# A second expert tile prepared during attention, and the expert totals moved behind a quarter of a layer

## The chip, the core and the metric

The kernel runs on one core of one Trainium2 chip. The metric is the device time of one execution in microseconds. Its parts are named as in the profile: PE (TensorE's matmuls) and PEld (its weight loads), DVE (VectorE), ACT (ScalarE), POOL (GpSimd) and SP (SyncE), which issues most DMA transfers.

## What is computed

Attention with pooled queries, followed by a mixture of experts of which each token takes one:

```python
B, H, S, D = 8, 8, 1152, 64
q_pool = q.reshape(B, H, S // 2, 2, D).mean(axis=3)
scores = matmul(q_pool, k.T) / sqrt(D)
attn = softmax(scores)                      # max subtracted, exp, sum
x = matmul(attn, v)  ->  4608 tokens x 512
logits = x @ w_gate                         # 8 experts
e = argmax(logits);  gate = softmax(logits)[e]
eom = sigmoid(x @ w_output_gate)[e]
out = gate * eom * (relu(x @ w1[e]) @ w2[e])    # 512 -> 1024 -> 512
```

## The kernel before

**Attention** walks over 32 pairs of heads (8 batches of 4 pairs) in an order written out by hand for PE, DVE, ACT and POOL. When a batch of 576 tokens is complete, its router runs in small steps spread between the matmuls (`router`, L396 to L486): it takes the argmax, works out each token's slot in its expert's list, adds the batch's counts to `cum` (L473), writes the rows of x to the DRAM table `xrows` (L461, L462) and scatters the tokens' ids into the DRAM lists `idscr`, one list for each expert (L477). For the last batch this router is the end of attention: nothing is left to hide it, and its chain of small DVE operations runs from L323 through L377, L389 and L414 to L473.

**One tile ahead.** A tile is up to 256 tokens of one expert. Behind the router of the sixth batch (`b == nb - 3`, L485) `setup` (L628) looks at the counts so far. It picks the fullest expert, which is sure to hold 256 tokens, and gathers the ids (L612) and rows (L623) of a full tile of that expert by indirect DMA on POOL. This is tile -1. `oh1` marks its expert, `es` holds its number for the weight load. The loads of two weight buffers are issued before attention ends: the buffer `raw1a`, `raw2a` takes the weights of that expert, read from a register, and the buffer `raw1b`, `raw2b` takes expert 0's weights, as a guess for tile 0 (L718 to L723). A set of weights is four transfers of 1024 KB.

**The experts** (`run`, L668). 22 tiles are run one after the other: tile -1, then tiles 0 to 20, sorted by expert. With these inputs the experts get 157, 587, 936, 411, 612, 525, 663 and 717 tokens. Three more tiles stand in a conditional tail (L917), which isn't reached. A tile (`tile_`, L870) goes through these steps, and inside the block of L905 PE, DVE and ACT keep the order in which it is written:

- four times: `split2` makes a quarter of the high and low parts of the second layer's weights (L739 on ACT, L740 on DVE); `l1` runs a quarter of the first layer: 24 matmuls (L764), the ReLU on ACT (L767), the remainder on DVE (L768); then one function of the list `todo` is run;
- the weights of tile t + 2 are loaded into the buffer that this tile used (`loads`, L725), on a condition: only where the expert of that buffer changes (`chg`);
- `split1` for the next tile (L733, L734), half of the second layer (`l2`, 24 matmuls, L776 to L778), the next tile's transposes (`xt`: L749 on PE, L751 on ACT, L752 on DVE), the other half of the second layer. Outputs are scaled on DVE (L782) and scattered by POOL (L783).

Outside that block and between it and attention, the framework orders by priority and readiness, so an instruction of the expert block can run between instructions of attention. The first tile's transposes have high priority (L898).

**The totals.** What tiles 0 and up hold depends on the final `cum`. `totals1` (L791) copies `cum` on DVE (L793) and sums it over the partitions by a matmul on PE (L795). `totals2` (L797) turns the counts into tile numbers, less the tile that was taken early. `totals3` (L825) makes each tile's expert (`ei`), the flags `chg` and the positions `ri` in the id lists (L839). `first` (L858) then gathers ids and rows for tiles 0 and 1 and issues the load of tile 0. `totals1` and `totals2` run ahead of tile -1, `totals3` and `first` behind its first two quarters.

Of the kernel before, what the change touches and what calls it, by code (L numbers as in the profile page):

```python
# [8 lines left out]
F32 = mybir.dt.float32  # L9
# [23 lines left out]
TS = 256  # L33
# [13 lines left out]
XW = 513  # L47
# [524 lines left out]
def keep_tiles(tc, kp, NT):  # L572
    nc = tc.nc
    k = {}

    def t(name, shape, dt):
        k[name] = kp.tile(shape, dt, name=name)
        return k[name]
    make_identity(nc, t('ident', [128, 128], F32))
    nc.vector.memset(t('ones', [128, 128], BF16), 1.0)  # L580
    nc.vector.memset(t('onesf', [128, 128], F32), 1.0)
    nc.gpsimd.iota(t('em8', [128, 5, 8], F32), pattern=[[0, 5], [1, 8]], base=-8, channel_multiplier=0, allow_small_or_imprecise_dtypes=True)
    nc.gpsimd.iota(t('Tn', [128, NT, 8], F32), pattern=[[1, NT], [0, 8]], base=0, channel_multiplier=0, allow_small_or_imprecise_dtypes=True)
    nc.gpsimd.iota(t('Tp', [128, NT, 2], F32), pattern=[[TS, NT], [128, 2]], base=0, channel_multiplier=1, allow_small_or_imprecise_dtypes=True)
    nc.gpsimd.iota(t('e46', [128, 8], F32), pattern=[[ESTRIDE, 8]], base=0, channel_multiplier=0, allow_small_or_imprecise_dtypes=True)
    t('oh1', [128, 8], F32)
    t('ef', [128, NT + 2], F32)
    t('es', [128, 1], I32)
    return k


class Moe:
    def __init__(self, tc, kp, keep, xrows, idscr, cum, w1, w2, out, nb):
        self.tc, self.kp, self.keep = tc, kp, keep
        self.xrows, self.idscr, self.cum, self.out = xrows, idscr, cum, out
        self.NTOK = nb * NQ
        self.early = max(nb - 2, 0) * NQ
        self.P1 = -(-self.early // 8) // TS
        self.NT = (self.NTOK - 8) // TS + 8 - self.P1
        assert self.P1 <= 1  # L600
        self.w1v = w1.rearrange("e (c p) f -> e p c f", p=128)
        self.w2v = w2.rearrange("e (c p) f -> e p c f", p=128)
        self.T = {}
        self.scat = []
# [14 lines left out]
    def gather(self, t, pool, bufs, rows):  # L619
        nc = self.tc.nc  # L620
        for j in range(2):
            xg = pool.tile([128, XW], F32, name="xg", bufs=2 * bufs)
            self.lastg = nc.gpsimd.indirect_dma_start(out=xg, out_offset=None, in_=self.xrows[0:rows],  # L623
                                         in_offset=bass.IndirectOffsetOnAxis(ap=self.T[t]['ids'][j][:, 0:1], axis=0),
                                         bounds_check=rows - 1, oob_is_err=False)
            self.T[t]['xg'].append(xg)

    def setup(self, psum):  # L628

        nc, kp, k, P1 = self.tc.nc, self.kp, self.keep, self.P1  # L630
        V = nc.vector
        if not P1:
            V.memset(k['oh1'], 0.0)
            V.memset(k['ef'][:, 0:2], 0.0)
            return
        cb = kp.tile([128, 8], BF16, name="cb1")
        V.tensor_copy(out=cb, in_=self.cum)
        yield
        yield 1
        cp = psum()  # L640
        nc.tensor.matmul(cp[:, 0:8], lhsT=k['ones'], rhs=cb, start=True, stop=True)
        cn = kp.tile([128, 8], F32, name="cn1")
        V.tensor_copy(out=cn, in_=cp[:, 0:8])
        yield
        mx = kp.tile([128, 1], F32, name="mx1")
        em = k['em8'][:, 0]
        V.tensor_reduce(out=mx, in_=cn, axis=AX.X, op=ALU.max)
        V.tensor_tensor(out=cn, in0=cn, in1=mx.broadcast_to([128, 8]), op=ALU.is_equal)
        yield
        V.tensor_tensor(out=cn, in0=cn, in1=em, op=ALU.mult)  # L650
        V.tensor_reduce(out=mx, in_=cn, axis=AX.X, op=ALU.min)
        yield
        V.tensor_scalar(out=k['ef'][:, 1:2], in0=mx, scalar1=8.0, scalar2=None, op0=ALU.add)
        V.tensor_tensor(out=k['oh1'], in0=em, in1=mx.broadcast_to([128, 8]), op=ALU.is_equal)
        V.memset(k['ef'][:, 0:1], 0.0)
        yield
        V.tensor_copy(out=k['es'], in_=k['ef'][:, 1:2])
        ri = kp.tile([128, 2], U32, name="ri1")
        rb = kp.tile([128, 1], F32, name="rb1")
        V.tensor_scalar(out=rb, in0=k['ef'][:, 1:2], scalar1=float(ESTRIDE), scalar2=None, op0=ALU.mult)  # L660
        V.tensor_tensor(out=ri, in0=k['Tp'][:, 0], in1=rb.broadcast_to([128, 2]), op=ALU.add)
        yield
        self.gather_ids(-1, ri, kp, 1)
        for _ in range(8):
            yield
        self.gather(-1, kp, 1, self.early)

    def run(self):  # L668
        tc, k, P1, NT = self.tc, self.keep, self.P1, self.NT
# [2 lines left out]
        with ExitStack() as ctx:  # L672
# [42 lines left out]
                        tc.add_manual_dep(d.ins, behind.ins.name, mybir.DependencyInfo(mybir.DependencyClass.Sync, mybir.DependencyReason.DATA), reason="small transfers first")  # L715
                return r[-1]

            if P1:  # L718
                e = nc.sync.value_load(k['es'][0:1, 0:1], min_val=0, max_val=7)
                wload(0, bass.ds(e, 1))  # L720
            else:
                wload(0, slice(0, 1))
            lastw = [wload(1, slice(0, 1))]  # L723

            def loads(t, **kw):  # L725
                with tc.issue_after(lastw[0].ins):
                    e = nc.sync.value_load(z['ei'][0:1, t:t + 1], min_val=0, max_val=7)
                    c = nc.sync.value_load(z['chg'][0:1, t:t + 1], min_val=0, max_val=1)
                    lastw[0] = wload((t + 1) % 2, bass.ds(e, 1), cond=c, cond_hint=False, **kw)

            def split1(t, c):
                raw = raw1[(t + 1) % 2]
                nc.scalar.copy(out=W1[0][:, c], in_=raw[:, c])  # L733
                V.tensor_tensor(out=W1[1][:, c], in0=raw[:, c], in1=W1[0].bitcast(F32)[:, c], op=ALU.subtract)  # L734

            def split2(t, c):
                z = slice(2 * c, 2 * c + 2)
                raw = raw2[(t + 1) % 2]
                nc.scalar.copy(out=W2[0][:, z], in_=raw[:, z])  # L739
                V.tensor_tensor(out=W2[1][:, z], in0=raw[:, z], in1=W2[0].bitcast(F32)[:, z], op=ALU.subtract)  # L740

# [55 lines left out]
            def totals2():  # L797
                cp = z['cp']
                ni = m1.tile([128, 8], I32, name="ni")
                V.scalar_tensor_tensor(out=ni, in0=k['oh1'], scalar=-float(TS) * P1, in1=cp[:, 0:8], op0=ALU.mult, op1=ALU.add)  # L800
                ns = m1.tile([128, 8], I32, name="ns")
                V.tensor_scalar(out=ni, in0=ni, scalar1=TS - 1, scalar2=None, op0=ALU.add)
                V.tensor_scalar(out=ns, in0=ni, scalar1=8, scalar2=None, op0=ALU.logical_shift_right)
# [11 lines left out]
                ts = z['ts'] = m1.tile([128, 8], F32, name="ts")  # L815
                V.tensor_tensor(out=ts, in0=te, in1=nt, op=ALU.subtract)
                eo = m1.tile([128, 8], F32, name="eo")
                V.scalar_tensor_tensor(out=eo, in0=k['oh1'], scalar=float(TS) * P1, in1=k['e46'], op0=ALU.mult, op1=ALU.add)
                vA = z['vA'] = m1.tile([128, 8], F32, name="vA")
                V.scalar_tensor_tensor(out=vA, in0=ts, scalar=-float(TS), in1=eo, op0=ALU.mult, op1=ALU.add)  # L820

# [34 lines left out]
                    self.gather(t, mg, 3, self.NTOK + 1)  # L856

            def first():  # L858
                for t in range(2):
                    gid(t)  # L860
                loads(0)
                for t in range(2):
                    gat(t)
                z['lg'] = self.lastg
                if not P1:
                    loads(1, behind=z['lg'])

            order = list(range(-P1, NT - SKIP))

# [23 lines left out]
            E = mybir.EngineType  # L893
            for c in range(4):
                split1(order[0], c)
            todo = [totals2, totals3, first]
            if P1:
                with tc.high_priority():  # L898
                    xt(order[0])
            else:  # L900
                totals1()
                while todo:
                    todo.pop(0)()
                xt(order[0])
            with tc.manual_schedule(engines={E.PE, E.DVE, E.Activation}):  # L905
                if P1:
                    totals1()
                    todo.pop(0)()
                for i, t in enumerate(order):
                    tile_(i, t, order[i + 1] if i + 1 < len(order) else None)  # L910
                pend.pop(0)()
# [5 lines left out]
            with tc.If(rv > NT - SKIP):  # L917
                for t in tail:
                    gid(t)
                    gat(t)  # L920
                    e = nc.sync.value_load(z['ei'][0:1, t:t + 1], min_val=0, max_val=7)
                    wload((t + 1) % 2, bass.ds(e, 1))
                    for c in range(4):
                        split1(t, c)
                    xt(t)
                    for c in range(4):
                        split2(t, c)
                    for g in range(4):
                        l1(t, g)
                    for j in range(2):  # L930
                        l2(t, j)()


def body(tc, qT, kT, vL, wg, w1, w2, out, nb=8):
    nc = tc.nc
    NTOK = nb * NQ
    with tc.tile_pool(name="dram", bufs=1, space=bass.MemoryType.DRAM) as dp, tc.tile_pool(name="keep", bufs=1) as kp:
# [6 lines left out]

        def init(i):
            if i == 0:
                dz = kp.tile([1, XW], F32, name="dz")
                nc.gpsimd.memset(dz, 0.0)
                nc.sync.dma_start(out=xrows[NTOK:NTOK + 1], in_=dz)
                nc.gpsimd.memset(di, NTOK)  # L950
# [39 lines left out]
```

## Time and profile before

| | us |
|---|---|
| median of 3 runs (1623.79 to 1625.01) | 1624.14 |
| profiled run | 1624.72 |
| its span, first to last instruction | 1622.7 |
| PE busy | 1533.1 |
| DVE, ACT, POOL busy | 1073.4, 1078.5, 996.3 |
| last matmul of the last router (L444) starts at | 1087.33 |
| first layer of tile -1 starts at | 1091.20 |
| first layer of tile 0 starts at | 1121.65 |

The mean granted TensorE clock was 0.986. In a line of a timeline stand the start in us from the span's start, the length in us (for several in a row, from the first to the end of the last), the engine, the line, the operation, the tile written and those read, the shape, the count, and in brackets how long the engine stood idle before and what ended it. A matmul's length is its passage through the array; how fast they follow one another is read from their starts. A line of waits gives who waited, for whom, the total, the count and the longest.

### The profile page before, as it was taken

The page shows a single profiled execution, that of the slowest core. Times are in us where ns is not written, and L with a number is a line of the kernel's source. Part 1 is how long each engine was busy: PE and PEld are TensorE (multiplying, and loading weights), DVE is VectorE, ACT ScalarE, POOL GpSimd, SP SyncE. Part 2 cuts the span into 40 slices and gives each one's busy share as a digit, 9 for nine tenths or more (in the row PEclk, how much of TensorE's full clock was granted, in tenths as well). Part 3 has the DMA queues.
Part 4 walks back from the last instruction along what each step waited for, and adds up shares of the span by engine and source line. Part 5 has one row for each costly group of instructions (what it writes and reads, how often), then busy time and mean ns, then how long its engine had stood idle before and what let it go on. Part 6 is the DMA issues. An engine that isn't in the chain of part 4 may idle for free. (4 is left out here: it accounts for less than half of the span.)

```text
span 1622.7 us, 42199 instructions
## 1 busy us (share of the span) xinstructions
PE 1533.1 (94%) x16618; PEld 1411.1 (87%) x16618; DVE 1073.4 (66%) x2222; ACT 1078.5 (66%) x1862; POOL 996.3 (61%) x917
## 2 busy tenths in 40 slices
PE   4999999999999999999999999879999999999997
PEld 4898889888988888888888888868999999999996
DVE  4676776776676676676677767656666566656663
ACT  2887778877878787878777877744445444544541
POOL 4887888788879788879788978634222322232300
PEclk9999999999999999999999999979999999999999
DMA  7765455655566457446645664255454655263600
GB/s 207 217 160 143 133 149 149 156 139 141 152 151 158 124 144 189 129 123 175 158 129 153 161 154 127 83 173 196 168 190 156 213 176 194 94 226 107 208 22 25
DMA packets 88754, 245.48 MB, mean 151 GB/s; under 512 B 13082, under 2 KB 17370, under 8 KB 88546
## 3 DMA queue, kind: packets, MB, share of 16 engines
q1 hardware_dynamic: 78826, 221.07, 48.6%
q0 software_dynamic: 9728, 21.67, 4.2%
q8 instruction: 134, 2.20, 0.6%
q14 instruction: 66, 0.54, 0.1%
HBM read 165.04 MB, written 23.81 MB: 116 GB/s over the span
## 5 line engine op out<-in xcount | busy, mean ns | idle before, releaser
L233 DVE TENSOR_REDUCE pm<-mp 128x1 f32<-128x384 f32 x864 | 457.6, 549 | 263.3 <-PE mp L232 257.7
L295 POOL TENSOR_TENSOR pl<-p,ph 128x576 f16<-128x576 f32 x381 | 490.2, 1287 | 187.8 <-ACT ph L294 155.5
L232 PE MATMUL mp<-ka,qa 128*128 128x384 f32 x960 | 317.7, 347 | 20.2 <-DMA qa<-yq 18.5
L293 ACT ACTIVATE p<-sps 128x576 f32<-128x576 f32 x381 | 251.0, 659 | 116.8 <-PE sps L281 108.3
L308 PEld LDWEIGHTS <-ph 128*128 128x128 f16 x2880 | 262.6, 97 | 74.3 <-DVE xb L323 40.8
L308 PE MATMUL av<-vt,ph 128*128 128x65 f16 x2880 | 297.0, 194 | 23.4 <-DVE xb L323 23.4
L279 PE MATMUL sps<-qa,ka 128*128 128x288 f32 x1152 | 281.6, 326 | 16.7 <-ACT ph L294 10.9
L309 PE MATMUL av<-vt,ph 128*128 128x64 f16 x2880 | 294.7, 195 | 0.0
L310 PE MATMUL av<-vt,pl 128*128 128x65 f16 x2880 | 293.8, 193 | 0.0
L309 PEld LDWEIGHTS <-ph 128*128 128x128 f16 x2880 | 266.2, 97 | 0.4
L310 PEld LDWEIGHTS <-pl 128*128 128x128 f16 x2880 | 266.5, 99 | 0.0
L232 PE MATMUL mp<-kb,qb 66*128 66x384 f32 x768 | 262.5, 342 | 0.6 <-DMA kb<-kp 0.6
L281 PE MATMUL sps<-qb,kb 68*128 68x288 f32 x1152 | 248.5, 298 | 2.8 <-DMA qb<-mr 2.8
L294 ACT ACTIVATE ph<-sps 128x576 f16<-128x576 f32 x381 | 249.3, 654 | 0.0
L279 PEld LDWEIGHTS sps<-qa,ka 128*128 128x128 f32 x1152 | 183.5, 191 | 27.9 <-ACT ph L294 19.2
L764 PE MATMUL hps<-xh,w1h 128*128 128x256 f32 x704 | 200.4, 285 | 0.0
L764 PE MATMUL hps<-xl,w1h 128*128 128x256 f32 x704 | 200.3, 284 | 0.0
L232 PEld LDWEIGHTS mp<-ka,qa 128*128 128x128 f32 x960 | 180.4, 192 | 22.8 <-issue 18.5
L764 PE MATMUL hps<-xh,w1l 128*128 128x256 f32 x704 | 199.6, 284 | 0.0
L767 ACT ACTIVATE hh<-hps 128x512 fp32r<-128x512 f32 x88 | 52.7, 598 | 221.1 <-PE hps L764 221.1
L285 ACT ACTIVATE ph<-sps 128x576 f16<-128x576 f32 x195 | 128.9, 661 | 92.0 <-PE sps L281 89.7
L281 PEld LDWEIGHTS sps<-qb,kb 68*128 68x128 f32 x1152 | 186.7, 191 | 3.2 <-DMA qb<-mr 3.2
(170 smaller groups left out, 3184.6 us busy)
## 6 DMA issues: line engine op xcount, KB each, us to landing
ka<-xk SPq DMA_DIRECT2D x128, 288.0 KB
raw1b<-in_w_dram SPq DMA_DIRECT2D x24, 1024.0 KB
raw2b<-in_w_dram SPq DMA_DIRECT2D x24, 1024.0 KB
raw1a<-in_w_dram SPq DMA_DIRECT2D x22, 1024.0 KB
raw2a<-in_w_dram SPq DMA_DIRECT2D x22, 1024.0 KB
qp<-in_qT_dram SPq DMA_DIRECT2D x32, 576.0 KB
kpf<-in_kT_dram SPq DMA_DIRECT2D x32, 576.0 KB
vp<-in_vL_dram SPq DMA_DIRECT2D x32, 576.0 KB
```

Source lines behind the costliest of these rows:

```text
L232: nc.tensor.matmul(mp, lhsT=l, rhs=r, start=j == 0, stop=j == len(ops) - 1)
L233: nc.vector.tensor_reduce(out=pm[:, i:i + 1], in_=mp, axis=AX.X, op=ALU.max)
L279: nc.tensor.matmul(sps[:, j, 0:288], lhsT=ka[:, h, ks], rhs=qa[:, o + 288 * j:o + 288 * j + 288], start=True, stop=False)
L281: nc.tensor.matmul(sps[:, j, 0:288], lhsT=kb[:, h, ks], rhs=qb[:, h, 288 * j:288 * j + 288], start=False, stop=True)
L285: nc.scalar.activation(out=ph2, in_=x, func=AF.Exp, scale=1.0 / 16)
L293: nc.scalar.activation(out=p32.rearrange("p (j n) -> p j n", j=2), in_=x, func=AF.Exp, scale=1.0 / 16)
L294: nc.scalar.activation(out=ph2, in_=x, func=AF.Exp, scale=1.0 / 16)
L295: nc.gpsimd.tensor_tensor(out=pl, in0=p32, in1=ph, op=ALU.subtract)
L308: nc.tensor.matmul(av_[:, qb, 0:65], lhsT=hi, rhs=vt[:, h, c, 0:65], start=c == 0 and qb == 0, stop=False)
L309: nc.tensor.matmul(av_[:, qb, 0:64], lhsT=hi, rhs=vt[:, h, c, 66:130], start=False, stop=False)
L310: nc.tensor.matmul(av_[:, qb, 0:65], lhsT=lo, rhs=vt[:, h, c, 0:65], start=False, stop=c == NC - 1 and qb == 4)
L764: nc.tensor.matmul(hp[:, f], lhsT=W1[w][:, c, fs], rhs=d[x][:, c], start=i == 0, stop=i == 11)
```

## The change

Two tiles, numbered -2 and -1, are prepared in attention. `setup` picks the fullest expert, takes 256 from its count, picks the fullest of what is left, and gathers ids and rows of both, each with eight steps between ids and rows. With these inputs they are experts 2 and 7. Both weight buffers are loaded by register, so the guess of expert 0 is gone, and tile 0's weights come by a conditional load like all others. That load, `loads(0)`, now stands at the end of tile -2's first layer and waits for the last gather that `first` issued. `first` gathers tile 0 alone. The numbers of tiles go from 24 to 23 in the tables, and the tiles run are -2 to 19, again 22, with the same contents in sum. `totals1` becomes the first entry of `todo`, so `totals1`, `totals2`, `totals3` and `first` stand behind the first, second, third and fourth quarter of tile -2's first layer. A row of zeros (`dz`) shares the buffers of the early rows.

```diff
-        self.P1 = -(-self.early // 8) // TS
+        self.P1 = sum(self.early - TS * i >= 8 * TS for i in range(2))
...
         cp = psum()
         nc.tensor.matmul(cp[:, 0:8], lhsT=k['ones'], rhs=cb, start=True, stop=True)
...
+        for i in range(2):
+            V.tensor_reduce(out=mx, in_=cn[i], axis=AX.X, op=ALU.max)
+            V.tensor_tensor(out=w, in0=cn[i], in1=mx.broadcast_to([128, 8]), op=ALU.is_equal)
+            yield
+            V.tensor_tensor(out=w, in0=w, in1=em, op=ALU.mult)
+            V.tensor_reduce(out=mx, in_=w, axis=AX.X, op=ALU.min)
+            yield
+            V.tensor_scalar(out=k['ef'][:, i:i + 1], in0=mx, scalar1=8.0, scalar2=None, op0=ALU.add)
+            V.tensor_tensor(out=oh[i], in0=em, in1=mx.broadcast_to([128, 8]), op=ALU.is_equal)
+            yield
+            if i == 0:
+                V.scalar_tensor_tensor(out=cn[1], in0=oh[0], scalar=-float(TS), in1=cn[0], op0=ALU.mult, op1=ALU.add)
...
-        self.gather_ids(-1, ri, kp, 1)
-        for _ in range(8):
-            yield
-        self.gather(-1, kp, 1, self.early)
+        for i in range(2):
+            self.gather_ids(i - 2, ri[i], kp, 2)
+            for _ in range(8):
+                yield
+            self.gather(i - 2, kp, 2, self.early)
+            yield
...
-            if P1:
-                e = nc.sync.value_load(k['es'][0:1, 0:1], min_val=0, max_val=7)
-                wload(0, bass.ds(e, 1))
-            else:
-                wload(0, slice(0, 1))
-            lastw = [wload(1, slice(0, 1))]
+            lastw = [None]
+            for i in range(2):
+                e = slice(0, 1)
+                if P1:
+                    e = bass.ds(nc.sync.value_load(k['es'][0:1, i:i + 1], min_val=0, max_val=7), 1)
+                lastw[0] = wload(i, e)
...
             def first():
-                for t in range(2):
+                for t in range(1 if P1 else 3):
                     gid(t)
-                loads(0)
-                for t in range(2):
+                for t in range(1 if P1 else 3):
                     gat(t)
                 z['lg'] = self.lastg
                 if not P1:
-                    loads(1, behind=z['lg'])
+                    loads(0)
+                    loads(1)
...
-            todo = [totals2, totals3, first]
+            todo = [totals1, totals2, totals3, first]
...
             with tc.manual_schedule(engines={E.PE, E.DVE, E.Activation}):
-                if P1:
-                    totals1()
-                    todo.pop(0)()
                 for i, t in enumerate(order):
                     tile_(i, t, order[i + 1] if i + 1 < len(order) else None)
```

More of the change, by code (lines that the diff above doesn't have):

```diff
@@ L587, in keep_tiles @@
     t('ef', [128, NT + 2], F32)
-    t('es', [128, 1], I32)
+    t('es', [128, 2], I32)
     return k
@@ L597, in __init__ @@
         self.early = max(nb - 2, 0) * NQ
-        self.P1 = -(-self.early // 8) // TS
+        self.P1 = sum(self.early - TS * i >= 8 * TS for i in range(2))
         self.NT = (self.NTOK - 8) // TS + 8 - self.P1
-        assert self.P1 <= 1
+        assert self.P1 in (0, 2)
         self.w1v = w1.rearrange("e (c p) f -> e p c f", p=128)
@@ L621, in gather @@
         for j in range(2):
-            xg = pool.tile([128, XW], F32, name="xg", bufs=2 * bufs)
+            xg = pool.tile([128, XW], F32, name="xg", tag="xg", bufs=2 * bufs)
             self.lastg = nc.gpsimd.indirect_dma_start(out=xg, out_offset=None, in_=self.xrows[0:rows],
@@ L641, in setup @@
         nc.tensor.matmul(cp[:, 0:8], lhsT=k['ones'], rhs=cb, start=True, stop=True)
-        cn = kp.tile([128, 8], F32, name="cn1")
-        V.tensor_copy(out=cn, in_=cp[:, 0:8])
+        cn = [kp.tile([128, 8], F32, name=f"cn{i}") for i in range(2)]
+        V.tensor_copy(out=cn[0], in_=cp[:, 0:8])
         yield
+        em = k['em8'][:, 0]
+        es8 = k['e46']
+        oh = [kp.tile([128, 8], F32, name=f"ob{i}") for i in range(2)]
+        w = kp.tile([128, 8], F32, name="cw")
         mx = kp.tile([128, 1], F32, name="mx1")
-        em = k['em8'][:, 0]
@@ L647, in setup @@
-        V.tensor_reduce(out=mx, in_=cn, axis=AX.X, op=ALU.max)
-        V.tensor_tensor(out=cn, in0=cn, in1=mx.broadcast_to([128, 8]), op=ALU.is_equal)
-        yield
-        V.tensor_tensor(out=cn, in0=cn, in1=em, op=ALU.mult)
-        V.tensor_reduce(out=mx, in_=cn, axis=AX.X, op=ALU.min)
-        yield
-        V.tensor_scalar(out=k['ef'][:, 1:2], in0=mx, scalar1=8.0, scalar2=None, op0=ALU.add)
-        V.tensor_tensor(out=k['oh1'], in0=em, in1=mx.broadcast_to([128, 8]), op=ALU.is_equal)
-        V.memset(k['ef'][:, 0:1], 0.0)
@@ L656, in setup @@
[L656 to L662, printed above, removed]
-        self.gather_ids(-1, ri, kp, 1)
-        for _ in range(8):
+        rb = kp.tile([128, 1], F32, name="rb1")
@@ new lines, in setup @@
+        ri = [kp.tile([128, 2], U32, name=f"ri{i}") for i in range(2)]
+        for i in range(2):
[10 more added lines that the diff above has]
+                V.scalar_tensor_tensor(out=cn[1], in0=oh[0], scalar=-float(TS), in1=cn[0], op0=ALU.mult, op1=ALU.add)
+                V.tensor_tensor(out=w, in0=oh[0], in1=es8, op=ALU.mult)
+            else:
+                V.scalar_tensor_tensor(out=w, in0=oh[0], scalar=float(TS), in1=es8, op0=ALU.mult, op1=ALU.add)
+                V.tensor_tensor(out=w, in0=oh[1], in1=w, op=ALU.mult)
+            yield
+            V.tensor_reduce(out=rb, in_=w, axis=AX.X, op=ALU.add)
+            V.tensor_tensor(out=ri[i], in0=k['Tp'][:, 0], in1=rb.broadcast_to([128, 2]), op=ALU.add)
+            yield
@@ L665, in setup @@
+        V.tensor_tensor(out=k['oh1'], in0=oh[0], in1=oh[1], op=ALU.add)
+        V.tensor_copy(out=k['es'], in_=k['ef'][:, 0:2])
+        yield
+        for i in range(2):
+            self.gather_ids(i - 2, ri[i], kp, 2)
+            for _ in range(8):
+                yield
+            self.gather(i - 2, kp, 2, self.early)
             yield
-        self.gather(-1, kp, 1, self.early)
     def run(self):
@@ L728, in loads @@
                     c = nc.sync.value_load(z['chg'][0:1, t:t + 1], min_val=0, max_val=1)
-                    lastw[0] = wload((t + 1) % 2, bass.ds(e, 1), cond=c, cond_hint=False, **kw)
+                    lastw[0] = wload(t % 2, bass.ds(e, 1), cond=c, cond_hint=False, **kw)
             def split1(t, c):
-                raw = raw1[(t + 1) % 2]
+                raw = raw1[t % 2]
                 nc.scalar.copy(out=W1[0][:, c], in_=raw[:, c])
@@ L737, in split2 @@
                 z = slice(2 * c, 2 * c + 2)
-                raw = raw2[(t + 1) % 2]
+                raw = raw2[t % 2]
                 nc.scalar.copy(out=W2[0][:, z], in_=raw[:, z])
@@ L799, in totals2 @@
                 ni = m1.tile([128, 8], I32, name="ni")
-                V.scalar_tensor_tensor(out=ni, in0=k['oh1'], scalar=-float(TS) * P1, in1=cp[:, 0:8], op0=ALU.mult, op1=ALU.add)
+                V.scalar_tensor_tensor(out=ni, in0=k['oh1'], scalar=-float(TS), in1=cp[:, 0:8], op0=ALU.mult, op1=ALU.add)
                 ns = m1.tile([128, 8], I32, name="ns")
@@ L817, in totals2 @@
                 eo = m1.tile([128, 8], F32, name="eo")
-                V.scalar_tensor_tensor(out=eo, in0=k['oh1'], scalar=float(TS) * P1, in1=k['e46'], op0=ALU.mult, op1=ALU.add)
+                V.scalar_tensor_tensor(out=eo, in0=k['oh1'], scalar=float(TS), in1=k['e46'], op0=ALU.mult, op1=ALU.add)
                 vA = z['vA'] = m1.tile([128, 8], F32, name="vA")
@@ L905, in run @@
             with tc.manual_schedule(engines={E.PE, E.DVE, E.Activation}):
-                if P1:
-                    totals1()
-                    todo.pop(0)()
                 for i, t in enumerate(order):
@@ L921, in run @@
                     e = nc.sync.value_load(z['ei'][0:1, t:t + 1], min_val=0, max_val=7)
-                    wload((t + 1) % 2, bass.ds(e, 1))
+                    wload(t % 2, bass.ds(e, 1))
                     for c in range(4):
@@ L946, in init @@
             if i == 0:
-                dz = kp.tile([1, XW], F32, name="dz")
+                dz = kp.tile([128, XW], F32, name="dz", tag="xg", bufs=4)[0:1]
                 nc.gpsimd.memset(dz, 0.0)
```

## The prediction

> **What bounds the kernel now.** I read the page first, for the span, then PE's waits in the expert part alone, then PE's, DVE's and ACT's timelines across the change-over from attention to experts.
>
> ```profile
> span 1622.7 us, 42199 instructions
> ```
>
> The profiled run took 1624.72 us, of which 1622.7 is the span, so 2.0 lie around it. It is 0.58 above the median of the runs, 1624.14.
>
> ```profile
> engine line waited for: us in total, times, longest us
> PE cp L795 <- DVE cb L793: 3.6, 1, 3.6
> PE xps L749 <- DMA xg<-xrows,ids: 2.4, 2, 1.6
> ```
>
> These are all the waits of PE from 1088 us to the end. The 22 tiles are bound by PE, and weights and splits cost nothing there. So what the change can win after attention lies in these two places, with the clock that drops around them. Both kernels run 22 tiles: by the counts of the inputs the eight experts fill 22 tiles however many full ones are taken early, and the conditional tail isn't reached. I take all later tiles as unchanged.
>
> ```profile
> 1091.15 0.19 PE L795 MATMUL cp<-cb,ones 128*128 128x8 bf16 x1 [3.63 <-DVE cb L793]
> 1091.20 0.56 PE L764 MATMUL hps<-xh,w1h 128*128 128x256 f32 x1
> 1091.56 0.41 PE L764 MATMUL hps<-xl,w1h 128*128 128x256 f32 x1
> ...
> 1096.25 0.41 PE L764 MATMUL hps<-xh,w1l 128*128 128x256 f32 x1
> 1096.46 0.41 PE L764 MATMUL hps<-xh,w1h 128*128 128x256 f32 x1
> ...
> 1105.42 0.40 PE L776 MATMUL yp<-w2h,hh 128*128 128x512 f32 x1
> ...
> 1111.81 0.66 PE L749 MATMUL xps<-ident,xg 128*128 128x128 f32 x4 [0.77 <-DMA xg<-xrows,ids]
> 1114.09 0.98 PE L749 MATMUL xps<-ident,xg 128*128 128x128 f32 x4 [1.62 <-DMA xg<-xrows,ids]
> ...
> 1121.65 0.28 PE L764 MATMUL hps<-xh,w1h 128*128 128x256 f32 x1
> ```
>
> The first tile: the totals' matmul, the first layer from 1091.20 (its second quarter begins at 1096.46), the second layer from 1105.42, the next tile's transposes with their two waits, the next tile from 1121.65.
>
> **Part 1: the totals move behind the first quarter.** The 3.63 us look like the prize. But what else held the first layer?
>
> ```profile
> 1089.68 1.28 DVE L752 TENSOR_TENSOR xl<-xps,xh 128x512 fp32r<-128x512 f32 x2
> 1090.87 0.22 DVE L793 COPY cb<-cum 128x8 bf16<-128x8 bf16 x1
> ```
> ```profile
> 1087.72 1.05 ACT L751 CAST xh<-xps 128x512 fp32r<-128x512 f32 x2
> ```
>
> The first tile's own `xl` is finished by DVE at 1089.68 + 1.28 = 1090.96, and every second matmul of the layer needs it or comes behind one that does. L793 ends at 1091.09 and L795 starts 0.06 later; with the same 0.06 behind `xl`, the layer's second matmul could start at 1091.02 in place of 1091.56. The first one needs only `xh`, ready at 1088.77, and goes ahead. Gain 0.54; if the first doesn't go ahead, 0.36 later, 0.18. I take 0.54.
>
> Now the price of the new place. In the written order of DVE the copy L793 stands behind L768 of the first quarter, which waits for ACT's L767, which waits for that quarter's 24 matmuls; and PE, in order, holds the second quarter behind L795.
>
> ```profile
> 1096.84 0.60 ACT L767 ACTIVATE hh<-hps 128x512 fp32r<-128x512 f32 x1 [8.06 <-PE hps L764]
> ```
> ```profile
> 1097.47 0.69 DVE L768 SCALAR_TENSOR_TENSOR hl<-hps,hh 128x512 fp32r<-128x512 f32 x1 [2.82 <-ACT hh L767]
> 1098.07 0.35 DVE L829 TENSOR_TENSOR ge<-Tn,tb 128x192 f32<-128x192 f32 x1
> ```
>
> The 24th matmul starts at 1096.25, L767 at 1096.84, L768 at 1097.47, the next DVE operation at 1098.07. With the copy there (0.22), the 0.06, and the 0.05 from L795 to the next matmul, the second quarter starts at 1098.40 instead of 1096.46: a new wait of 1.94 us. It depends on no cover that I could lose; all three links are in this trace. Behind PE's wait stands all of PE's queue; behind the copy on DVE stand only the totals and L740 of the next quarters, which l2 needs some 10 us later.
>
> DVE's first instruction of the expert block is now L740 of the first quarter, 1.23 us long, no longer held behind the totals. It may run before the router's end:
>
> ```profile
> 1077.09 1.03 ACT L739 CAST w2h<-raw2a 128x1024 fp32r<-128x1024 f32 x1
> 1082.02 0.76 ACT L374 CAST xh<-tp 128x256 fp32r<-128x256 f32 x3 [3.90 <-PE tp L370]
> ```
> ```profile
> 1080.94 0.49 DVE L323 TENSOR_TENSOR xb<-av,r 128x320 f32<-128x320 f32 x1
> 1082.43 0.95 DVE L377 TENSOR_TENSOR xl<-tp,xh 128x256 fp32r<-128x256 f32 x3 [0.99 <-ACT xh L374]
> 1093.42 1.23 DVE L740 TENSOR_TENSOR w2l<-raw2a,w2h 128x1024 fp32r<-128x1024 f32 x1
> ```
>
> ACT already does so: L739 of the tile runs ahead of the router's L374, in a stretch that was idle. In DVE's idle 0.99 before L377, L740 would delay the router's chain by 1.23 - 0.99 = 0.24; between two links of the chain by 1.23; behind L752 by nothing. I take 0.24, by ACT's example.
>
> **Part 2: the clock behind the new wait.** The stretches below give, behind their length, the busy time of PE, PEld, DVE, ACT and POOL, the granted clock, the DMA share and GB/s.
>
> ```profile
> 1090.27:1093.68 3.41, 2.53 (x12) 2.54 (x13) 2.88 (x17) 0.00 (x0) 2.78 (x3) 0.50 1.03 250
> 1093.68:1097.10 3.42, 3.42 (x17) 3.42 (x17) 0.97 (x1) 0.26 (x1) 2.50 (x2) 0.50 0.22 55
> 1097.10:1100.51 3.41, 3.41 (x30) 3.41 (x30) 2.81 (x10) 1.93 (x4) 0.00 (x0) 0.98 0.01 1
> ```
>
> The clock changes here on a grid of 3.41 us. The stretch with PE busy for 2.53 did not bring full clock, the one with 3.42 did. Matmuls go at 0.213 us at half clock (1091.56 to 1096.46 holds 23).
>
> ```profile
> 1565.01 0.28 PE L764 MATMUL hps<-xh,w1h 128*128 128x256 f32 x1
> 1576.52 0.40 PE L776 MATMUL yp<-w2h,hh 128*128 128x512 f32 x1
> 1588.32 0.28 PE L764 MATMUL hps<-xh,w1h 128*128 128x256 f32 x1
> ```
>
> At full clock the layer's 96 take 11.51, 0.120 each. So each us at half clock costs 1 - 0.120 / 0.213 = 0.44. The changed kernel resumes at about 1096.46 - 0.54 + 0.24 + 1.94 = 1098.1; before, only the 0.64 from 1096.46 to 1097.10 were slow (0.28 lost). On this grid full clock comes at 1100.51 or 1103.92, after 2.4 or 5.8 us: 0.77 or 2.27 more lost than before. If instead the first quarter already brings full clock, about nothing is lost. Where the grid falls differs from run to run, so I take 1.2 between 0 and 2.3. [...]
>
> **Part 3: two tiles in attention.** The second prepared tile needs no gather at the change-over. From the second layer's start to the next tile the profile has 1121.65 - 1105.42 = 16.23, against 1588.32 - 1576.52 = 11.80 late in the run: 4.43 go, the two waits and the half clock they brought. What is late next? The gather for tile 0, now needed one tile later, at about 1137 us:
>
> ```profile
> 1100.34 0.21 DVE L839 TENSOR_TENSOR ri<-A,Tp 128x48 uint32<-128x48 f32 x1
> ```
> ```profile
> ids<-idscr,ri POOLq DMA_INDIRECT x44, 2.4
> xg<-xrows,ids POOLq DMA_INDIRECT x44, 3.7
> ```
>
> The positions were ready at 1100.34; with the totals one piece and one wait later, I put them at about 1111; two id gathers, two row gathers and a landing (some 8 us) make it 1119. Expert 0's weights, loaded statically before and now read behind that gather, start then:
>
> ```profile
> 1117.58:1120.99 3.41, 3.41 (x17) 2.81 (x16) 1.23 (x1) 1.05 (x1) 2.66 (x3) 0.98 0.98 336
> ```
>
> At 336 GB/s their 4.2 MB (four transfers of 1024 KB) need 12.5 us, so 1131.5, when the splits of that tile begin at about 1132 and its first layer at 1143. The load is hidden, and slack is left if it takes half as long again.
>
> In attention the change adds four indirect transfers on POOL and some 13 small DVE operations.
>
> ```profile
> 765.16:800.16 35.00, 33.80 (x457) 31.52 (x456) 24.27 (x56) 28.84 (x56) 28.20 (x25) 1.00 0.60 151
> 895.00:930.00 35.00, 33.80 (x455) 31.28 (x455) 26.00 (x65) 28.77 (x56) 31.92 (x28) 1.00 0.64 163
> ```
>
> The second stretch holds today's preparation, the first is the same place one batch earlier: PE's 33.80 is equal. Cost 0, covered by POOL's and DVE's slack.
>
> **Sum:** -0.54 + 0.24 + 1.94 + 1.2 - 4.43 = -1.6. Ends: -0.54 + 0 + 1.94 + 0 - 4.43 = -3.0, and -0.18 + 1.23 + 1.94 + 2.3 - 4.43 = +0.9. Against the profiled run 1623.1; its 0.58 above the median taken off, **1622.5** (1621.1 to 1625.0).
>
> **Rivals.**
>
> *The totals' wait is not paid.* DVE stands idle for 2.82 us ahead of L768; a copy placed there would be done before the quarter ends. Against it: in the trace DVE runs the block in its written order. Without 1.94 and 1.2 the sum is -4.7: 1619.4.
>
> *POOL becomes the bound of attention during the longer preparation.*
>
> ```profile
> 906.08 1.13 POOL L612 DMA_INDIRECT ids<-idscr,ri  x1 [0.16 <-PE mp L232]
> 907.51 1.00 POOL L612 DMA_INDIRECT ids<-idscr,ri  x1 [0.31 <-issue]
> 919.73 1.10 POOL L623 DMA_INDIRECT xg<-xrows,ids  x1 [0.15 <-issue]
> 921.13 1.00 POOL L623 DMA_INDIRECT xg<-xrows,ids  x1 [0.30 <-issue]
> ```
>
> Four more take 4.2 us and their gaps 0.9, and POOL has 35.00 - 31.92 = 3.1 left. Should `pl` come so late that PE waits for all of it, +5.1 - 1.6 = +3.5: 1627.6, slower. It decides once the backlog outgrows the nine `ph` and `pl` buffers. Against: the first four cost PE nothing, and POOL has the following batch to catch up.
>
> *The change removes a wait that wasn't one and the waits come back.* If DVE, with the totals now among the quarters, hands over `hl` late, l2 of the first tile waits; I find it done within half a us of its need. One to two us more: 1624, no change.
>
> **How the numbers follow.** My forecast has 0.70, the unpaid wait 0.14, POOL 0.07, late `hl` 0.09. A measurement here can tell about 0.2%, 3.2 us: under 1620.9 counts as faster, over 1627.4 as slower. Faster: 0.14 and the low edge of my case, 0.21. Slower: POOL and what I haven't seen, 0.09. The range takes my case's ends, the unpaid wait with the spread of the runs, and not POOL: 1619.0 to 1625.6.
>
> **What would show it.** Right: PE's wait for `cb` at L795 is about 1.9 us in place of 3.6, and stands behind 24 matmuls; no wait of L749 for `xg`; a stretch of half clock behind L795. The first layer begins within 0.6 us of 1091.2, the third tile at about 1143. Wrong: no wait at L795, PE waits for `pl`, `w1l` or `w2l`, or a change in attention's length of more than 1 us.

## The result, and the profile after

The changed kernel takes 1638.09 us (median of 5 runs, 1632.80 to 1642.10) where the kernel before takes 1623.80 (5 runs, 1622.62 to 1625.01). The ratio is 1.0072, 95% interval 1.0056 to 1.0088: slower by some 11.7 us by the ratio (the two medians lie 14.3 apart). The prediction was 1622.5.

The profiled run took 1634.43 us, 9.7 more than that of before. Where do they come from? First the page, then, of the waits of PE from 60 to 1080 us, the one that stands out (us in total, times, longest):

```profile
span 1632.6 us, 42200 instructions
```
```profile
PE mp L232 <- DVE pm L233: 10.2, 2, 8.7
```

In the kernel before the same line reads

```profile
PE mp L232 <- DVE pm L233: 1.6, 1, 1.6
```

So there is one wait of 8.7 us in the middle of attention, in which PE, busy for 1534.3 of the 1632.6 us and so the engine that bounds the kernel, does nothing. It lies at 940 us, where the first of the two tiles is gathered. The instructions of POOL, DVE and PE there (changed kernel; in brackets the idle time ahead of an instruction and what ended it):

```profile
934.02 1.02 POOL L623 DMA_INDIRECT xg<-xrows,ids  x1
935.34 1.00 POOL L623 DMA_INDIRECT xg<-xrows,ids  x1 [0.30 <-issue]
936.37 1.29 POOL L295 TENSOR_TENSOR pl<-p,ph 128x576 f16<-128x576 f32 x1
937.59 0.24 POOL L150 CAST qd<-xq 64x64 fp32r<-64x64 f32 x1
942.77 0.24 POOL L150 CAST qd<-xq 64x64 fp32r<-64x64 f32 x1 [4.94 <-DMA xg<-xrows,ids]
943.50 1.03 POOL L612 DMA_INDIRECT ids<-idscr,ri  x1 [0.49 <-POOL qd L150]
944.83 1.00 POOL L612 DMA_INDIRECT ids<-idscr,ri  x1 [0.30 <-DMA qb<-mr]
945.89 1.27 POOL L295 TENSOR_TENSOR pl<-p,ph 128x576 f16<-128x576 f32 x1
947.25 0.24 POOL L182 TENSOR_SCALAR inv<-ex 128x2 f32<-128x2 f32 x1
...
947.53 0.17 DVE L184 RECIPROCAL sc<-inv 128x2 f32<-128x2 f32 x1 [10.05 <-POOL inv L182]
...
948.20 0.69 PE L232 MATMUL mp<-ka,qa 128*128 128x384 f32 x1 [8.66 <-DVE pm L233]
```

Read it from the bottom. PE waits because its `mp` buffers aren't drained; DVE drains them (L233) but stands in its order at L184; L184 needs POOL's `inv` (L182); and ahead of L182 POOL had two row gathers of tile -2, 4.94 us of standing still for one of these gathers to land, and two id gathers of tile -1. The same place in the kernel before:

```profile
934.41 0.53 POOL L150 CAST qd<-xq 64x64 fp32r<-64x64 f32 x2
935.19 1.28 POOL L295 TENSOR_TENSOR pl<-p,ph 128x576 f16<-128x576 f32 x1 [0.25 <-POOL qd L150]
936.57 0.24 POOL L182 TENSOR_SCALAR inv<-ex 128x2 f32<-128x2 f32 x1
...
936.84 0.17 DVE L184 RECIPROCAL sc<-inv 128x2 f32<-128x2 f32 x1
```

Here L150's two casts run as a pair, L182 comes at once, and L184 has no bracket: DVE didn't wait. Nor had it time to spare, since L182 ended at 936.81 and L184 began at 936.84.

The granted clock falls in the idle time, from 1.00 in the first of these rows to 0.50. The columns are the length, the busy time and count of PE, PEld, DVE, ACT and POOL, the granted clock, the DMA share and GB/s (changed kernel):

```profile
936.90:940.30 3.40, 2.64 (x31) 2.40 (x27) 0.54 (x3) 2.27 (x5) 0.93 (x2) 1.00 0.99 246
940.30:943.70 3.40, 0.00 (x0) 0.00 (x0) 0.00 (x0) 0.47 (x1) 0.44 (x2) 0.93 1.05 244
943.70:947.10 3.40, 0.00 (x0) 0.00 (x0) 0.00 (x0) 0.00 (x0) 3.03 (x3) 0.50 0.69 171
947.10:950.50 3.40, 2.30 (x20) 2.00 (x21) 2.79 (x7) 0.78 (x1) 3.23 (x5) 0.50 0.00 0
950.50:954.00 3.50, 3.50 (x23) 3.35 (x23) 2.15 (x5) 2.43 (x5) 1.57 (x2) 0.57 0.00 0
```

PE works again from 948.2, but at a granted clock of 0.50 up to about 953.5 (0.57 is the mean of the last row).

At the end of attention DVE shows a second loss, L754 (L740 of before) between two links of the last router:

```profile
1092.49 0.23 DVE L317 TENSOR_SCALAR r<-av,sc 128x5 f32<-128x5 f32 x1 [3.46 <-PE av L310]
1092.69 1.22 DVE L754 TENSOR_TENSOR w2l<-raw2a,w2h 128x1024 fp32r<-128x1024 f32 x1
1093.84 0.18 DVE L320 RECIPROCAL r<-r 128x5 f32<-128x5 f32 x1
```

1093.84 - 1092.69 = 1.15 us. Then the change-over, with the lines that answer to those of before (PE, changed kernel):

```profile
1100.31 0.19 PE L444 MATMUL tp<-cum,ones 128*128 128x40 bf16 x1
...
1103.99 0.58 PE L778 MATMUL hps<-xl,w1h 128*128 128x256 f32 x1 [1.60 <-DVE xl L766]
1109.98 0.18 PE L809 MATMUL cp<-cb,ones 128*128 128x8 bf16 x1 [1.63 <-DVE cb L807]
1118.72 0.40 PE L790 MATMUL yp<-w2h,hh 128*128 128x512 f32 x1
1130.57 0.28 PE L778 MATMUL hps<-xh,w1h 128*128 128x256 f32 x1
```

The last router's matmul L444 starts 1100.31 - 1087.33 = 12.98 later than before. From there to the second tile's first layer the changed kernel takes 30.26 us in place of 34.32: 4.06 are won. From the second tile to the end of the span it takes 502.03 in place of 501.05. 12.98 - 4.06 + 0.98 = 9.9, the difference of the spans. So the change-over gained, and attention lost three times as much.

### The profile page after: what moved, and what is told of

It reads as the page before. It is cut to its first block, busy times and chain, and to the rows that moved or that the text cites. A ratio compares the mean times of both kernels' runs of the same rounds, so it can differ in the third digit from the quotient of the medians.

```text
span 1632.6 us, 42200 instructions
## 1 busy us (share of the span) xinstructions
PE 1534.3 (94%) x16618; PEld 1411.3 (86%) x16618; DVE 1075.8 (66%) x2234; ACT 1078.5 (66%) x1862; POOL 991.0 (61%) x917
## 5 line engine op out<-in xcount | busy, mean ns | idle before, releaser
L233 DVE TENSOR_REDUCE pm<-mp 128x1 f32<-128x384 f32 x864 | 456.7, 548 | 261.2 <-PE mp L232 255.8
L295 POOL TENSOR_TENSOR pl<-p,ph 128x576 f16<-128x576 f32 x381 | 489.7, 1286 | 190.4 <-ACT ph L294 156.9
L232 PE MATMUL mp<-ka,qa 128*128 128x384 f32 x960 | 318.5, 348 | 29.0 <-DMA qa<-yq 18.7
L232 PE MATMUL mp<-kb,qb 66*128 66x384 f32 x768 | 262.8, 342 | 0.6 <-DMA kb<-kp 0.6
L232 PEld LDWEIGHTS mp<-ka,qa 128*128 128x128 f32 x960 | 180.2, 192 | 32.7 <-issue 18.9
```

Source lines behind the costliest of these rows:

```text
L232: nc.tensor.matmul(mp, lhsT=l, rhs=r, start=j == 0, stop=j == len(ops) - 1)
L233: nc.vector.tensor_reduce(out=pm[:, i:i + 1], in_=mp, axis=AX.X, op=ALU.max)
L295: nc.gpsimd.tensor_tensor(out=pl, in0=p32, in1=ph, op=ALU.subtract)
```

## The experiments

Theory A: a cast of L150 stands still while an indirect gather is open, and all that stands on POOL ahead of L182 reaches PE. Theory B: POOL simply hasn't the time for four more transfers. The intervals below are 95%, against the kernel before on the same chip.

**The row gathers four steps earlier** (changed kernel):

```diff
-            for _ in range(8):
+            for _ in range(8 if i else 4):
                 yield
             self.gather(i - 2, kp, 2, self.early)
-            yield
+            for _ in range(1 if i else 5):
+                yield
```

> The changed kernel, with the row gathers of tile -2 issued 4 steps behind its id gathers in place of 8, and the steps taken away added behind them, so that all the rest of the preparation keeps its place; nothing is added or left out. Theory A (a pair of POOL instructions of attention, L150, is held until an open gather has landed, and the new gathers of tile -2 stand right ahead of it): with some four steps between gather and L150 the 4.94 us of POOL's wait and the 8.7 us of PE's wait behind it go, the last router's L444 comes near 985 and 1089 us in place of 995.62 and 1100.31, and the time falls by about 10 to 1623 to 1626 us. Theory B (POOL has not the room for four more indirect transfers): their number is the same, so the time stays at 1633 to 1638 us, and L444 stays near 1100.

Measured: 1630.68 us (10 runs, 1627.63 to 1633.89), ratio 1.0030 (1.0018 to 1.0042). L444 at 1095.11. The rows of POOL, DVE and PE:

```profile
938.38 0.52 POOL L150 CAST qd<-xq 64x64 fp32r<-64x64 f32 x2
939.24 1.03 POOL L612 DMA_INDIRECT ids<-idscr,ri  x1 [0.34 <-POOL qd L150]
940.58 1.00 POOL L612 DMA_INDIRECT ids<-idscr,ri  x1 [0.30 <-PE sps L281]
...
943.00 0.24 POOL L182 TENSOR_SCALAR inv<-ex 128x2 f32<-128x2 f32 x1
...
943.27 0.17 DVE L184 RECIPROCAL sc<-inv 128x2 f32<-128x2 f32 x1 [5.02 <-POOL inv L182]
...
943.95 0.44 PE L232 MATMUL mp<-ka,qa 128*128 128x384 f32 x1 [3.61 <-DVE pm L233]
```

The wait of L150 is gone, the casts run as a pair. Yet PE still waits 3.61. Neither theory holds as it was put: A said that all 10 us would go, B that none would. Both have a part. The four transfers, about 1.2 us each with their gaps, all stand ahead of L182 here.

**The kernel before with its one row gather seven steps later:**

```diff
-        for _ in range(8):
+        for _ in range(15):
             yield
         self.gather(-1, kp, 1, self.early)
```

> The kernel before, with its one row gather 15 steps behind the id gathers in place of 8, so that it stands right ahead of the instructions L295 and L150 of POOL; one tile as before, no transfer more. Theory A (an open gather holds L150): the wait of L150 and the wait of PE behind it appear although only one tile is prepared, 5 to 11 us longer, 1629 to 1635 us. Theory B (the load of four more transfers on POOL): nothing is added here, 1624 us.

Measured: 1631.41 us (5 runs, 1630.30 to 1634.93), ratio 1.0038 (1.0023 to 1.0053), some 6 us longer without a single transfer more.

```profile
935.47 1.00 POOL L623 DMA_INDIRECT xg<-xrows,ids  x1 [0.30 <-issue]
936.50 1.28 POOL L295 TENSOR_TENSOR pl<-p,ph 128x576 f16<-128x576 f32 x1
937.73 0.23 POOL L150 CAST qd<-xq 64x64 fp32r<-64x64 f32 x1
942.61 0.23 POOL L150 CAST qd<-xq 64x64 fp32r<-64x64 f32 x1 [4.65 <-DMA xg<-xrows,ids]
```

By place alone a part of the changed kernel's loss, some 6 us of 11.7, has come into the kernel before. As the only cause, B is out.

**One step later still.** The row gather now stands behind both casts, still ahead of L182.

```diff
-        for _ in range(8):
+        for _ in range(16):
```

> The kernel before with its one row gather one step later than in the earlier run with 15 steps: 16 steps behind the ids, which puts it behind both instructions L150 and ahead of L182. Theory A: no wait of L150 any more (4.65 us there), but two transfers still ahead of L182, 2.4 us; L182 is late by about 2 to 3 us and PE's wait for pm is 1.6 to 3 us: 1625 to 1628 us. Rival (POOL stalls for an open gather at whatever comes next): the 5 us and the time of that run, 1630 us or more.

Measured: 1625.37 us (10 runs, 1622.94 to 1628.69), ratio 1.0010 (1.0000 to 1.0020).

```profile
932.81 0.52 POOL L150 CAST qd<-xq 64x64 fp32r<-64x64 f32 x2
933.71 1.10 POOL L623 DMA_INDIRECT xg<-xrows,ids  x1 [0.38 <-POOL qd L150]
935.11 1.00 POOL L623 DMA_INDIRECT xg<-xrows,ids  x1 [0.30 <-issue]
936.17 1.28 POOL L295 TENSOR_TENSOR pl<-p,ph 128x576 f16<-128x576 f32 x1
937.54 0.24 POOL L182 TENSOR_SCALAR inv<-ex 128x2 f32<-128x2 f32 x1
```

One step in the order of POOL is worth 0.28% here (1.0038 to 1.0010), some 4.5 us. L295 and L182 run right behind the gathers with no wait. The trace has no landing for these two gathers. In the run before the cast stood for its gathers until 942.61, 7.1 us behind the start of the second one (935.47); by that these two were still open. In the changed kernel, too, L295 and the first cast ran (936.37 and 937.59) while the second cast stood for the gather until 942.77. So POOL as such isn't held; of its work here only the second cast is. The two transfers alone make L182 late by 2.66 (DVE's idle time) and PE by 1.27.

**All eight transfers, spread out** (changed kernel): behind L182, or a pair of heads later.

```diff
-            for _ in range(8):
+            for _ in range(11 if i else 12):
                 yield
             self.gather(i - 2, kp, 2, self.early)
-            yield
+            for _ in range(6):
+                yield
```

> The changed kernel with the second tile's transfers spread out in attention: row gathers of tile -2 twelve steps behind its ids (behind L150 and L182 of POOL in place of ahead of them), ids of tile -1 six steps later, its rows eleven steps behind those, behind the next pair's L182; all eight transfers stay and the totals stay at the change's place. Theory A (what counts is only what stands on POOL ahead of L182, an open gather or transfers): the waits of PE for pm go back to the 1.6 us of before, L444 of the last batch starts within 2 us of 1088.5 (1.15 of it the slip of L754), and the time is 1623 to 1628 us. Theory B (the four more transfers cost POOL their time wherever they stand): L444 stays 5 us or more late, 1629 us or more.

Measured: 1624.70 us (12 runs, 1621.59 to 1628.35), ratio 1.0005 (0.9995 to 1.0015). L444 at 1090.37.

```profile
937.60 0.24 POOL L182 TENSOR_SCALAR inv<-ex 128x2 f32<-128x2 f32 x1
939.37 1.10 POOL L623 DMA_INDIRECT xg<-xrows,ids  x1 [0.16 <-PE tp L385]
...
937.88 0.17 DVE L184 RECIPROCAL sc<-inv 128x2 f32<-128x2 f32 x1
```

POOL does the same work, L184 has no bracket again, and nearly the whole loss of the change is gone: 1.0072 to 1.0005. Up to L444 it is 2.9 behind the kernel before (table below), 1.15 of it the slip of the making of `w2l`; where the other 1.7 lie wasn't found. POOL had the time; it didn't have it ahead of L182.

The six kernels side by side (idle times at this one place; the last column is the start of the last batch's L444 less that of its first record, at about 205 us):

| | ahead of L182 on POOL | DVE ahead of L184 | PE ahead of L232 | to L444 |
|---|---|---|---|---|
| before | none | 0 | 0 | 882.4 |
| one gather, 16 steps | 2 transfers | 2.66 | 1.27 | 883.1 |
| changed, 4 steps earlier | 4 transfers | 5.02 | 3.61 | 889.3 |
| one gather, 15 steps | 2 transfers, open gather | 7.07 | 5.67 | 891.0 |
| changed | 4 transfers, open gather | 10.05 | 8.66 | 895.1 |
| changed, spread | none | 0 | 0 | 885.3 |

The terms add up: an open gather adds 4.4 to two transfers and 5.0 to four. PE's wait is 1.4 us shorter than DVE's each time, which is what its buffers cover. From 3.6 us on, L444 is later than PE's wait alone explains: with one gather, 15 steps, by 2.9 (891.0 - 882.4 - 5.67); in the changed kernels, measured from the spread one, which has the slip and the other 1.7 as well, by 0.4 and 1.1 (889.3 - 885.3 - 3.61 and 895.1 - 885.3 - 8.66). The granted clock of 0.50 behind PE's wait, shown above, may be the reason; no run separated it.

**The totals alone** (kernel before, one tile):

```diff
-            todo = [totals2, totals3, first]
+            todo = [totals1, totals2, totals3, first]
...
-                if P1:
-                    totals1()
-                    todo.pop(0)()
```

> The kernel before with the totals alone moved: the copy of the counts and its matmul stand behind the first quarter of the first tile's first layer; one tile is prepared as before, so attention keeps its length up to the last router. Theory A (the new place costs what the terms say): L740 slips into the router +1.2, start of the first layer -0.5, new wait of PE +1.6 to 1.9, clock 0 to 2.3, and the gathers for tile 0 come about 5 us later, so the two waits for xg, 2.4 us before, grow by some 3 to 5: 1628 to 1634 us. Theory B (the totals' place is free, PE's wait of 3.63 was the price): 1622 to 1624 us.

Measured: 1635.25 us (4 runs, 1632.86 to 1638.77), ratio 1.0060 (1.0038 to 1.0082), a little more than expected. Of PE's waits from 1080 us on:

```profile
PE xps L749 <- DMA xg<-xrows,ids: 8.1, 2, 7.4
PE tp L370 <- DVE xb L323: 2.1, 1, 2.1
...
PE cp L795 <- DVE cb L793: 1.6, 1, 1.6
```

Theory B of this run is out. The 3.63 us became 1.6 at another place, the router's wait for `xb` grew from 1.1 to 2.1 by the slip of L740, and the gathers for tile 0, issued a quarter later, made PE wait 8.1 in place of 2.4. With one prepared tile the move costs more than it saves.

**The copy back ahead of the block** (changed kernel; only `cb` moves, its matmul stays behind the quarter):

```diff
-            def totals1():
-                cb = m1.tile([128, 8], BF16, name="cb")
+            def totals0():
+                cb = z['cb'] = m1.tile([128, 8], BF16, name="cb")
                 V.tensor_copy(out=cb, in_=self.cum)
+
+            def totals1():
+                cb = z['cb']
...
             with tc.manual_schedule(engines={E.PE, E.DVE, E.Activation}):
+                if P1:
+                    totals0()
```

> The changed kernel with the copy of the counts (cb) put back ahead of the block, first thing on DVE, while its matmul stays behind the first quarter. Theory A (the copy's place on DVE makes both PE's wait of 1.63 us at the totals' matmul and the slip of the 1.2 us long making of w2l between two links of the router): both go, the half clock behind the wait too, 2.8 to 4 us less than the changed kernel, with the 10 us of attention still there: 1631 to 1635 us. Rival (the wait is the matmul's and its place's own, and the slip comes from priorities of the block): no more than 0.5 us less.

Measured: 1631.91 us (5 runs, 1631.81 to 1632.82), ratio 1.0038 (1.0024 to 1.0053). By the ratios that is 0.34%, some 5.5 us, less than the changed kernel. It is more than the expected 2.8 to 4, but the two intervals together leave some 3.5 us on either side, so that it is more than expected isn't shown.

```profile
1107.08 0.23 PE L812 MATMUL cp<-cb,ones 128*128 128x8 bf16 x1
```

No bracket: the wait of 1.63 is gone, and the wait for `xb` is 1.07 as before, so L754 no longer slips. One DVE instruction of 0.22 us, put first, holds DVE's part of the block behind the router, since it reads the final counts.

**Both mended:** the spread preparation and the copy ahead, the diffs of the two together.

> The same spread preparation, and the copy of the counts ahead of the block on DVE, its matmul behind the first quarter. If the costs found so far are all there are: against the kernel before, attention 0 to +1.5, change-over -4.7 (34.32 from L444 to the second tile's first layer before, 29.59 with the copy ahead), so 1620 to 1623 us where the kernel before takes 1624 to 1626; against the same kernel with the copy behind the quarter about 3 us less and with less spread between runs. Rival (the loss of 10 us in attention is more than the transfers' places): no faster than the kernel before.

Measured: 1621.88 us (12 runs, 1620.32 to 1624.00), ratio 0.9985 (0.9977 to 0.9994), which is faster than the kernel before by 0.15%, some 2.4 us, and by the medians 2.8 less than with the copy behind the quarter (1624.70).

**The second tile without the move of the totals:** the spread preparation, with `totals1` and `totals2` ahead of the block as before.

```diff
-            todo = [totals1, totals2, totals3, first]
+            todo = [totals2, totals3, first]
...
             with tc.manual_schedule(engines={E.PE, E.DVE, E.Activation}):
+                if P1:
+                    totals1()
+                    todo.pop(0)()
```

> The same spread preparation of two tiles, but the totals (copy, matmul and the counts' arithmetic) ahead of the first tile's block as in the kernel before; so it is the second tile alone, without the move of the totals. Expected by the terms: PE's wait of 3.63 for the copy stays, no wait for xg, so 4.4 less than the kernel before, 1619 to 1622 us, and within 1 us of the version with the copy ahead. Rival (the move of the totals is what brings the gain): 1623 us or more, as before.

Measured: 1622.42 us (12 runs, 1619.10 to 1624.10), ratio 0.9986 (0.9976 to 0.9996). The move of the totals, even with the copy ahead, brings nothing that shows: the ratio is 0.9985 with it and 0.9986 without, each within 0.1%. The gain is the second tile's: about 2.3 us, half of what I expected. In its profile, L444 to the second tile takes 29.18 against 34.32, so 5.1 are won; L444 itself is 1.5 later by the measure of the table, and the stretch from the second tile to the end 1.0 longer. The latter shows in all profiles with two tiles (0.8 to 1.2 against before). Some 0.6 of it are spread over the 20 tiles behind the second one, 23.36 us each in place of 23.33; why stays unexplained.

## Why the prediction was wrong, point by point

**Attention: "Cost 0, covered by POOL's and DVE's slack". This step failed.** It cost 12.7 us up to L444: 1.15 are the slip, 9.8 lie at the one place ahead of L182 (they go when the transfers are spread, 895.1 to 885.3), and 1.7 remain that no run placed. The step weighed busy time over 35 us: 31.92 of 35.00 on POOL. But slack in a stretch isn't slack ahead of one instruction, and the stretch that it took ends at 930, ahead of the place where the gathers came to stand. In the kernel before POOL stands idle for only 0.25 us in the last 8 ahead of L182, and behind L182 hang DVE's order and PE. Also, I costed the four transfers that are added and not the ones that are moved: seven more steps in the choice of tiles put the ids of the first tile at 918.42 in place of 906.08, and its rows at 934.02 in place of 919.73, from a place with cover to the one place without. At the 1.7 us of a step (eight from 906.08 to 919.73) a shift of some 12 us could have been worked out from rows that I quoted; L150 and L182, where it leads, weren't among them. That a cast waits for an open gather no row of before showed. The bounds of this term should have reached up to PE's standing still for a gather's landing. The prediction's own sign of being wrong, a change in attention's length of more than 1 us, is what came.

**The rival "POOL becomes the bound"** had POOL, and its +5.1 is near the 5.02 by which four transfers without an open gather make L184 late. But its road was the `pl` buffers, and its test, the backlog, was the wrong one: it came through `inv`, with PE's buffers giving cover for 1.4 us only.

**Start of the first layer, -0.54: right.** The matmul with `xl` starts 3.68 behind L444 in place of 4.23: -0.55.

**The slip of L740, 0.24: wrong.** It measured 1.15, near my upper bound of 1.23: it took the place between two links, not the idle one.

**The new wait, 1.94: right in kind.** It measured 1.63 and stands behind 24 matmuls as said.

**The clock, 1.2 between 0 and 2.3: the bounds were too narrow.** From the matmul with `xl` to the second layer the kernel before takes 13.86 and the changed kernel 14.73. Without the wait of 1.63 that is 0.76 less: the granted clock rose from 0.50 at about 1107.08, ahead of the wait. The run with the earlier gathers has the same wait, and these rows:

```profile
1098.78 0.58 PE L779 MATMUL hps<-xl,w1h 128*128 128x256 f32 x1 [1.59 <-DVE xl L767]
1105.68 0.19 PE L810 MATMUL cp<-cb,ones 128*128 128x8 bf16 x1 [1.63 <-DVE cb L808]
1117.12 0.40 PE L791 MATMUL yp<-w2h,hh 128*128 128x512 f32 x1
```

From the first to the last of these rows are 18.34 us, so +2.85 in the same working. The two other profiles with this wait have 14.72 (the spread preparation) and 15.66 (the totals alone), so -0.8 and +0.2. In the run with the earlier gathers the granted clock rose from 0.50 only at about 1111.84, behind the wait: it lies somewhat above the 2.3, as the changed kernel's profile lies below the 0. I take this difference to be one reason for the spread of the changed kernel (9.3 us over 5 runs, against 1.0 with the copy ahead and no wait; of the two spread versions 6.8 with the wait against 3.7 without, 12 runs each); that wasn't separated by a run.

**The waits for `xg`, -4.43: right.** Second layer to the next tile takes 11.85 in place of 16.23: -4.38. No wait for `xg` is left, and tile 0's weights came in time.

**The sum** without attention was -1.6; the spread version, which has these terms and the 1.7 and 1.0 us that no row explains, came out at +0.05% (-0.05 to +0.15%), about +0.8 us. With the slip at its size the sum is -0.7, just within that interval.

## What to carry to other kernels

A step that is moved costs what hangs on the instructions it now stands ahead of, so find for each engine in order the instruction that another engine is waiting for, and count what is queued ahead of that one; a busy share over a stretch can't tell. When a chain is made longer, work out where all that follows it will fall, and look at what stands there. And where a block has a written order, the first instruction of it on each engine decides how early the block may start running into what comes before it.

## What the runs showed of the hardware

A cast on POOL of 64 partitions, the second of two that are alike, waited 4.0 to 4.9 us for an open indirect gather in three kernels, while L295 and the first cast behind the same gathers didn't wait. Why the built program has that wait the traces don't show, and no kernel without it was tried.

In the changed kernel's profile, read from stretches of 1 us, the granted clock changed among others at 943.24, 953.48, 1066.12 and 1107.08 us, which lie 3, 33 and 12 times 3.413 us apart. These are the stretches of 1 us in which it rose from 0.50, in the changed kernel and in the run with the earlier gathers:

```profile
1107.00:1108.00 1.00, 1.00 (x10) 1.00 (x10) 0.00 (x0) 0.00 (x0) 0.92 (x1) 0.96 0.26 54
```
```profile
1111.00:1112.00 1.00, 1.00 (x7) 1.00 (x7) 0.14 (x1) 0.77 (x2) 0.00 (x0) 0.58 0.00 0
```

By the means of 0.96 and 0.58 it rose at about 1107.08 and 1111.84. In the changed kernel PE had worked from 1103.99, 3.1 us. In the run with the earlier gathers PE worked for 5.3 us from 1098.78 without a break, and all stretches of 1 us there show 0.50; this is the one at the end of that work:

```profile
1103.00:1104.00 1.00, 1.00 (x5) 0.76 (x4) 0.00 (x0) 0.00 (x0) 0.97 (x1) 0.50 0.04 8
```

After the wait of 1.63 it worked again from 1105.68, 6.2 us up to the rise. That later rise goes with the +2.85 of this run. Why 3.1 us of work came before the rise in the one and 5.3 us brought none in the other, no run separated.
